# Streamed columns, low parts and sums in the first third of a fused attention and token-mixer kernel

## The chip, the cores and the metric

The kernel runs on one core of one Trainium2 chip. The metric is the device time of one execution in microseconds (us); smaller is better. A core has five engines that run side by side and wait for each other by semaphores: TensorE (PE in the profile, with its weight loads shown as PEld), VectorE (DVE), ScalarE (ACT), GpSimd (POOL) and SyncE (SP, which here only issues DMAs). Each engine works through its own instructions in the order in which the program wrote them.

## The reference

One block of two parts with adaptive layer norms, on x of 2048 tokens by 448 features, all in fp32:

```python
mod = (silu(c) @ w_mod).reshape(6, 448)          # sa, ca, ga, sb, cb, gb
h = layernorm(x) * (1 + ca) + sa
q, k, v = h @ wqkv                               # 16 heads of 28
phi = lambda t: where(t > 0, t + 1, exp(t)) + 1e-6
kv = einsum("hsd,hse->hde", phi(k), v);  z = phi(k).sum over tokens
o = phi(q) @ kv / (phi(q) . z + 1e-6)
x = x + ga * (o @ wo)
h = layernorm(x) * (1 + cb) + sb
u = gelu(einsum("sd,sf->df", layernorm(h), w1) + b1)   # mixes over tokens
x = x + gb * (einsum("df,fs->sd", u, w2) + b2)
```

## The kernel before

The tokens are cut into 16 tiles of 128 (NT = 16). To keep fp32 accuracy on TensorE, a matrix is split into a high part, rounded to the short format fp32r, and a low part, the rest. A product is then three matmuls: high by high, high by low, low by high. The helper `split` makes both: ScalarE copies to fp32r (line L79 of the profile), VectorE subtracts (L80).

The work in the order of the program:

- **Start.** The modulation columns `1 + ca` and `sa` are made first, since they scale the weights. `col_mm` (L211) does this on TensorE: a piece of `w_mod` is the stationary operand, and one column of 128 numbers (a part of silu(c), or a column of ones) is streamed past it. `col_out` (L218) copies the result out of PSUM. `keep_warm` (L176) runs matmuls whose result nobody reads. `w_high` and `w_low` scale the projection weights and split them.
- **The pipeline over tiles**, after some tiles done by hand ahead of it: a loop over t from 4 to 15. On TensorE an iteration holds `project(t+1)` (ten matmuls, x by the scaled key weights), `close(t)` (an eleventh that brings in mean and shift), a small transpose for tile t+1, `a_outer(t-4)` (eleven matmuls that add up normed x by phi(k) in four PSUM banks `cacc`), and from t = 10 on `a_q` (a query projection). For these the other engines make: the parts `hh`, `hl` of transposed x (`a_split(t+3)`), the statistics of a tile (`a_stats(t+3)`), exp and relu of the keys (`a_exp(t)`, tiles `ek`, `rk`), `pk` (`a_pk(t)`, L400), its parts `pkh`, `pkl` (`a_pk_parts(t-1)`, L454 to L465), the normed x `xn` and its parts `xh`, `xl` (`a_high(t-2)`, `a_low(t-2)`, L435 to L443). The four parts of a scaled query weight are made in iterations 4 to 8 too (`w_high(0, ..)`, `w_low(0, ..)`, `row_part(0, ..)`).
- **Low parts by DMA.** For tiles 2 to 12, `pkl` and `xl` are not made by VectorE: ScalarE writes minus the high part, and a DMA issued on POOL adds the full tile to it in memory (`accum_op=ALU.add`). The helper `low` (L426) holds that choice for `xl`.
- **The sum of phi(k)** over tiles goes into two tiles, `pksum[0]` and `pksum[1]`. Tiles 2, 4, .. 12 (`SUM_DMA`) are added to the first by a DMA on POOL (L463), the others to the second by VectorE (L465).
- **Behind the loop** come the last `a_outer` calls, `zp` (two matmuls that turn the summed phi(k), split as `zh`, `zl`, into z), `zb` (its copy by ScalarE), `csum` (L654, L655), `kvb` (L664), the query projections left over, then the normalized attention output and the two token-mixing products, which fill the time from about 125 us to the end.

Most tiles live in one pool of 74 slots in SBUF (`slot`), handed out again in the order in which they came free; who writes a tile waits for the last reader of the slot's tile before. A second pool of 27 (`tslot`) lies behind the constants, so that the size of the unused constant `space` moves it. `moving` takes a tile's columns from 16 on, so that the streamed operands begin 64 bytes into their slot. In the program as built, the slots begin at byte 1152 of a partition, the second pool at byte 170304. `load_x` and `load_xt` fetch x and its transposed form; iteration t issues those of tile t+5.

Of the kernel before, what the change touches and what calls it, by code (L numbers as in the profile page):

```python
# [8 lines left out]
F32 = mybir.dt.float32  # L9
# [5 lines left out]
P = 128  # L15
# [12 lines left out]
Q_EARLY = {10: 0, 11: 1, 12: 2, 13: 3, 14: 4}  # L28
ACT_STATS = range(5)
RING = 6  # L30
SUM_DMA = (2, 4, 6, 8, 10, 12)
ROWS = 98
DVE_LOW = (0, 1, 13, 14, 15)
AHEAD = 8
# [13 lines left out]
def block_kernel(ctx: ExitStack, tc: tile.TileContext, x, xt, wqkv, wo, w1, b1, w2, b2, c, wmod, wfirst, out):  # L48
# [16 lines left out]
    def slot(name, w=D, dt=F32, parts=P):  # L65
        return slots.tile([parts, w], dt, name=name, tag="slot", padded_shape=[P, 512])
# [11 lines left out]
    def split(full, hi, lo):  # L78
        nc.scalar.activation(hi, full, AF.Copy)  # L79
        nc.vector.tensor_sub(lo, full, hi.bitcast(F32))  # L80
# [12 lines left out]
                            pattern=[[0, 4], [-DH, 4], [0, DH]], channel_multiplier=1)  # L93
    nc.gpsimd.affine_select(out=m3, in_=m3, compare_op=ALU.is_ge, fill=0.0, base=DH - 1,
                            pattern=[[0, 4], [DH, 4], [0, DH]], channel_multiplier=-1)
    cst.tile([P, 96], F32, name="space")
    mhalf = cst.tile([P, 2], F32, name="mhalf")
    nc.vector.memset(mhalf, -0.5)
    roots = cst.tile([P, 2], F32, name="roots")
# [20 lines left out]
    def load_x(t):  # L120
        X[t] = slot(f"x{t}")
        nc.sync.dma_start(X[t], xf[t * P:(t + 1) * P, :])
# [53 lines left out]
    def keep_warm(n):  # L176
        for i in range(n):
            nc.tensor.matmul(warm[:, :P], ones, ones, start=True, stop=True)
# [30 lines left out]
                                           op0=ALU.mult, op1=ALU.add)  # L209

    def col_mm(ps, a, b, first, last):  # L211
        for ch in range(4):
            n = P if ch < 3 else 64
            nc.tensor.matmul(ps[:n, ch:ch + 1], a[:, ch * P:ch * P + n], b, start=first and ch == 0, stop=last,
                             skip_group_check=True)
        nc.tensor.matmul(ps[64:, 3:4], a[:, 384:D], b, start=False, stop=last, skip_group_check=True)

    def col_out(j, ps):  # L218
        col[j] = cst.tile([P, 4], F32, name=f"col{j}")
        if j == 1:  # L220
            nc.vector.tensor_scalar_add(col[j], ps[:, :4], 1.0)
        else:
            nc.vector.memset(col[j], 0.0)
            nc.vector.tensor_copy(col[j][:, :3], ps[:, :3])
            nc.vector.tensor_copy(col[j][:64, 3:4], ps[:64, 3:4])
# [92 lines left out]


    heads, mv, xn = {}, {}, {}  # L320

    def b_square(src, nm, acc, name):
        junk = slot(f"sq{name}")
        nc.scalar.activation(junk, src, AF.Square, bias=nm, accum_out=acc)

    def a_stats(t):
        mv[t] = cst.tile([P, 3], F32, name=f"mv{t}")
        ve = small.tile([P, 2], F32, name=f"ve{t}", tag="ve")
        if t in ACT_STATS:
            junk = slot(f"ja{t}")  # L330
            sm = small.tile([P, 3], F32, name=f"as{t}", tag="as")
            nc.scalar.activation(junk, X[t], AF.Identity, accum_out=sm[:, 0:1])
            nc.scalar.activation(sm[:, 1:2], sm[:, 0:1], AF.Copy, scale=-1.0 / D)
            b_square(X[t], sm[:, 1:2], sm[:, 2:3], f"s{t}")
            nc.gpsimd.tensor_scalar_mul(mv[t][:, 0:1], sm[:, 0:1], 1.0 / D)
            nc.gpsimd.tensor_scalar(ve, sm[:, 2:3].to_broadcast([P, 2]), 1.0 / D, EPS, op0=ALU.mult, op1=ALU.add)
            nc.gpsimd.tensor_tensor(mv[t][:, 1:3], ve, roots, op=ALU.pow)
            return
        b6 = small.tile([P, 6], F32, name=f"st{t}", tag="st")
        nc.vector.bn_stats(b6, X[t])  # L340
        nc.vector.bn_aggr(mv[t][:, 0:2], b6)
        nc.vector.tensor_scalar_add(ve, mv[t][:, 1:2].to_broadcast([P, 2]), EPS)
        nc.gpsimd.tensor_tensor(mv[t][:, 1:3], ve, roots, op=ALU.pow)
# [11 lines left out]
    def a_transpose(t0, n=1):  # L355
        ps = bank(f"rw{t0}")
        for i in range(n):
            tps[t0 + i] = ps[:, i * P:(i + 1) * P]
            nc.tensor.transpose(tps[t0 + i][:ROWS], rowst[(t0 + i) % RING][:, :ROWS].bitcast(F32), ident)

    def a_copy(t):
        nc.scalar.activation(heads[t][1][64:ROWS, 384:], tps.pop(t)[64:ROWS], AF.Copy)

    def a_split(t):
        heads[t] = (slot(f"hh{t}", 512, F32R), slot(f"hl{t}", 512, F32R))
        split(XT[t], *heads[t])
        XT[t] = None

    pps = {}

# [21 lines left out]
    def a_exp(t, ps):  # L392
        eks[t] = (slot(f"ek{t}"), slot(f"rk{t}"))
        nc.scalar.activation(eks[t][0], ps, AF.Exp, scale=mv[t][:, 2:3])
        nc.scalar.activation(eks[t][1], ps, AF.Relu, scale=mv[t][:, 2:3])
# [27 lines left out]
    xss, pks = {}, {}  # L423
    pksum = []

    def low(t, lo, full, hi):  # L426
        if t in DVE_LOW:
            nc.vector.tensor_sub(lo, full, hi.bitcast(F32))
        else:
            nc.scalar.activation(lo, hi.bitcast(F32), AF.Copy, scale=-1.0)  # L430
            nc.gpsimd.dma_start(lo, full, accum_op=ALU.add)

    def a_high(t):
        h = slot(f"xn{t}")
        nc.vector.tensor_scalar(h, X[t], mv[t][:, 0:1], mv[t][:, 2:3], op0=ALU.subtract, op1=ALU.mult)  # L435
# [4 lines left out]
    def a_low(t):  # L440
        h = xn.pop(t)
        hi, lo = xss[t]
        nc.vector.tensor_sub(hi[:, D:], h[:, 384:D], hi[:, 384:D].bitcast(F32))  # L443
        low(t, lo, h[:, :384], hi[:, :384])

    pkf = {}

    def a_pk(t, ps):
        pkf[t] = phi_k(t, ps, tslot if t < 2 else slot)

    def a_pk_parts(t):
        pk = pkf.pop(t)
        hi, lo = moving(slot, f"pkh{t}"), moving(slot, f"pkl{t}")
        nc.scalar.activation(hi, pk, AF.Copy, bias=1e-6)  # L454
        if t in DVE_LOW:
            nc.vector.scalar_tensor_tensor(lo, pk, 1e-6, hi.bitcast(F32), op0=ALU.add, op1=ALU.subtract)  # L456
        else:
            nc.scalar.activation(lo, hi.bitcast(F32), AF.Copy, scale=-1.0, bias=1e-6)
            nc.gpsimd.dma_start(lo, pk, accum_op=ALU.add)
        if t < 2:  # L460
            pksum.append(pk)
        elif t in SUM_DMA:
            nc.gpsimd.dma_start(pksum[0], pk, accum_op=ALU.add)  # L463
        else:
            nc.vector.tensor_add(pksum[1], pksum[1], pk)  # L465
        pks[t] = (hi, lo)
# [20 lines left out]
    col_acc(1)  # L487
    a_split(0)
    col_mm(pc, macc.pop(1), one, False, True)
    keep_warm(2)  # L490
    col_out(1, pc)
    for ch in range(4):
        w_high(1, ch)
# [30 lines left out]
    a_stats(5)  # L524
    row_out(1)
    a_transpose(2, 2)
    project(4, 1, "kp")
    a_high(0)
    a_copy(2)
# [26 lines left out]
    for t in range(4, NT):  # L556
        if t + 1 < NT:
            project(t + 1, 1, "kp")
        kp = close(t, 1)
        if t + 1 < NT:  # L560
            a_transpose(t + 1)
        if t == 9:
            row_sum(0)
            row_bias(0)
        a_outer(t - KV_LAG)
        if t in Q_EARLY:
            a_q(Q_EARLY[t])
        if t == 12:
            mp = mod_sum2(2)
        if 4 < t < NT - 2:  # L570
            a_rows(t + 2)
        if 5 <= t < 9:
            w_low(0, t - 5)
            row_part(0, t - 5)
        if 7 < t + 3 < NT:
            a_stats(t + 3)
        a_phi_q(t in Q_EARLY)
        if t + 1 < NT:
            a_copy(t + 1)
        a_exp(t, kp)  # L580
        a_pk_parts(t - 1)
        highs = HIGH_AT.get(t, (t - 2,))
        for i in highs[:1]:
            a_high(i)
        a_pk(t, kp)
        for i in highs[1:]:
            a_high(i)
        for i in highs:
            a_low(i)
        if t + 3 < NT:  # L590
            a_split(t + 3)
        if 4 <= t < 8:
            w_high(0, t - 4)
        if t == 9:
            row_out(0)
        if t == 12:
            mod_out(2, mp)
        if t + 5 < NT:
            load_x(t + 5)
            load_xt(t + 5)  # L600
        if 7 <= t < 11:
            mod_part(2, t - 7)
        if t == 11:
            mod_split(2)
        for j, i in MOD_AT.get(t, ()):
            mod_part(j, i)
        if t == 5:
            load_mod(2)
        if t in (7, 9):
            load_mod(4 if t == 7 else 3)  # L610
        if t == 10:
            load_qkv(2, tslot)
        if t == 8:
            for g in range(4):
                w = tslot(f"wo{g}", parts=G)
                nc.sync.dma_start(w, wo[g * G:(g + 1) * G, :])
                wo_sb.append(w)
            b1c = cst.tile([P, NF], F32, name="b1c")
            nc.sync.dma_start(b1c, b1)
            b2c = cst.tile([P, NT], F32, name="b2c")  # L620
            nc.sync.dma_start(b2c, b2)
        if t >= 13:
            nc.vector.tensor_mul(wo_sb[t - 13], wo_sb[t - 13], mods[2][:G])
        load_to(PRE_LOAD.get(t, 0))
# [12 lines left out]
        mod_part(3, i)  # L637
    split_to(2)
    a_outer(NT - 2)
    zp = bank("zp")  # L640
    for i, pk in enumerate(zs):
        nc.tensor.matmul(zp[:, :D], ones_r, pk, start=(i == 0), stop=(i == 1))
    a_outer(NT - 1)
    zb = tslot("zb")
    nc.scalar.activation(zb, zp[:, :D], AF.Copy, bias=S * 1e-6)
    mod_split(4)
# [564 lines left out]
```

## Time and profile before

| what | value |
|---|---|
| time, median of 3 runs | 459.51 us (458.79 to 460.73) |
| time of the profiled execution | 459.63 us |
| its span, first to last instruction | 457.9 us |
| so around the span | 1.7 us |
| mean granted TensorE clock | 0.989 |
| busy: TensorE, VectorE, ScalarE, GpSimd | 445.3, 350.7, 274.7, 114.4 us |

How to read it: a row of the timeline gives start, duration, engine, line, operation, output<-inputs, shape, and in brackets how long the engine had sat idle and who ended that. Matmuls overlap in the record: one of 448 columns shows about 0.36 us, and the next begins about 0.20 us after it, so the distance between starts is what counts. The view of stretches gives for each window its length, the busy time of PE, PEld, DVE, ACT and POOL with the number of instructions, the granted clock, the share of the DMA engines' time that was busy, and GB/s. The view of waits gives who waited for whom, in total us, times, and the longest. The chain is the work that ended last, followed back, in order of time: start, us, what.

### The profile page before, as it was taken

Reading aid. Unit: us, or ns where it says so; the run is one execution under the profiler, and the core shown is the slowest. Engines: PE = TensorE matmul, PEld = TensorE weight load, DVE = VectorE, ACT = ScalarE, POOL = GpSimd, SP = SyncE. Lnnn points to the kernel's source line nnn. Section 1 sums busy time; section 2 is a strip of 40 time slices with the busy share of each in tenths; the row PEclk is TensorE's granted clock in tenths of the full one; section 3 lists DMA queues with packets and bytes.
Section 4 is the critical chain, followed back from the end, with each engine's and each line's share of the span. In section 5 each row is a group of like instructions: output and inputs, shape, how many; then the busy total and the mean of one; then the engine's idle time right before and its main releaser. Section 6 shows DMA issues by size and latency. Waiting matters only on the chain.

```text
span 457.9 us, 7383 instructions
## 1 busy us (share of the span) xinstructions
PE 445.3 (97%) x2364; PEld 409.0 (89%) x2364; DVE 350.7 (77%) x783; ACT 274.7 (60%) x596; POOL 114.4 (25%) x213
## 2 busy tenths in 40 slices
PE   8987899999999999999999999999999999999996
PEld 7865689998989999999999999999999999999996
DVE  3777887758999889988549766739696878978872
ACT  4888887775775676767665453426564446446531
POOL 3536554430003345444510000000100202302101
PEclk8899899999999999999999999999999999999999
DMA  7957999667300001422324544326895958967333
GB/s 263 379 164 164 212 255 280 100 121 235 110 1 1 1 23 25 116 49 47 83 100 153 178 158 149 100 87 192 254 236 113 195 168 175 217 164 143 52 87 61
DMA packets 59718, 64.25 MB, mean 140 GB/s; under 512 B 5344, under 2 KB 50208, under 8 KB 59680
## 3 DMA queue, kind: packets, MB, share of 16 engines
q1 hardware_dynamic: 51616, 51.17, 36.1%
q0 software_dynamic: 8064, 12.62, 17.5%
q8 instruction: 18, 0.29, 0.3%
q14 instruction: 20, 0.16, 0.1%
HBM read 46.57 MB, written 7.34 MB: 118 GB/s over the span
## 4 chain that ended last, share of the span: by engine, by line
PE 91%; ACT 3%; DMA 3%; DVE 1%; issue 1%; SPq 0%; POOL 0%
PE y L967 14%; PE up L775 10%; PE up L777 10%; PE up L776 10%; PE op L724 9%; PE qp L383 7%; PE y L968 7%; PE cacc L480 7%; PE kp L383 6%; PE yp L775 2%; PE yp L777 2%; PE yp L776 2%; PE tq L708 2%; DMA xl<-xn 1%; DMA xt<-in_xt_dram 1%
## 5 line engine op out<-in xcount | busy, mean ns | idle before, releaser
L775 PE MATMUL up<-h2h,ph 128*128 128x448 f32 x224 | 81.4, 363 | 0.0
L777 PE MATMUL up<-h2h,pl 128*128 128x448 f32 x224 | 81.2, 363 | 0.0
L776 PE MATMUL up<-h2l,ph 128*128 128x448 f32 x224 | 80.8, 361 | 0.0
L79 ACT ACTIVATE ph<-pr 128x512 fp32r<-128x512 f32 (+1 forms) x60 | 32.9, 569 | 24.0 <-PE up L776 17.7
L80 DVE TENSOR_TENSOR pl<-pr,ph 128x512 fp32r<-128x512 f32 (+1 forms) x60 | 36.3, 615 | 14.2 <-ACT ph L79 10.3
L777 PEld LDWEIGHTS up<-h2h,pl 128*128 128x128 f32 x224 | 42.0, 188 | 3.2
L776 PEld LDWEIGHTS up<-h2l,ph 128*128 128x128 f32 x224 | 42.0, 187 | 3.0
L775 PEld LDWEIGHTS up<-h2h,ph 128*128 128x128 f32 x224 | 42.1, 188 | 2.5
L929 POOL DMA_DIRECT2D a<-a x12 | 10.7, 936 | 114.2 <-PE yp L777 96.9
L987 POOL DMA_DIRECT2D out_dram<-yt x12 | 10.5, 874 | 81.8 <-DVE yt L978 53.5
L383 PE MATMUL kp<-wh,hh 128*128 128x448 f32 x64 | 25.1, 398 | 1.6 <-ACT hh L79 1.0
L480 PE MATMUL cacc<-pkh,xh 128*128 128x448 f32 x64 | 24.9, 389 | 0.7 <-ACT pkh L454 0.7
L973 ACT ACTIVATE cc<-y 128x448 f32<-128x448 f32 x18 | 9.8, 546 | 24.9 <-PE y L968 24.9
L724 PE MATMUL op<-wph,pth 112*128 112x448 f32 x64 | 24.7, 385 | 0.0
L480 PE MATMUL cacc<-pkl,xh 128*128 128x448 f32 x64 | 23.9, 374 | 0.2 <-DVE pkl L456 0.2
L383 PE MATMUL qp<-wh,hh 128*128 128x448 f32 x64 | 23.5, 367 | 0.0
L724 PE MATMUL op<-wpl,pth 112*128 112x448 f32 x64 | 23.4, 365 | 0.0
L724 PE MATMUL op<-wph,ptl 112*128 112x448 f32 x64 | 23.4, 365 | 0.0
L480 PE MATMUL cacc<-pkh,xl 128*128 128x448 f32 x48 | 18.0, 375 | 3.6 <-DMA xl<-xn 3.6
L712 ACT ACTIVATE pth<-tq 112x512 fp32r<-112x512 f32 x16 | 9.6, 600 | 19.6 <-PE tq L708 19.6
L775 PE MATMUL yp<-uw,qw 128*128 128x448 f32 x54 | 19.9, 369 | 0.0
L777 PE MATMUL yp<-uw,qw 128*128 128x448 f32 x54 | 19.7, 364 | 0.0
(246 smaller groups left out, 1329.2 us busy)
## 6 DMA issues: line engine op xcount, KB each, us to landing
pr<-in_B_w_dram SPq DMA_DIRECT2D x48, 256.0 KB, 3.0
a<-in_B_w_dram SPq DMA_DIRECT2D x24, 256.0 KB, 5.0
a<-in_B_w_dram SPq DMA_DIRECT2D x24, 192.0 KB, 5.1
xt<-in_xt_dram SPq DMA_DIRECT2D x16, 256.0 KB, 4.9
x<-in_A_x_dram SPq DMA_DIRECT2D x16, 224.0 KB, 4.5
wm<-in_B_wmod_dram SPq DMA_DIRECT2D x16, 196.0 KB, 4.8
wr<-in_qkv_dram SPq DMA_DIRECT2D x12, 224.0 KB, 5.4
out_dram<-x SPq DMA_DIRECT2D x12, 224.0 KB, 2.0
```

The lines of the kernel that those rows point to most:

```text
L79: nc.scalar.activation(hi, full, AF.Copy)
L80: nc.vector.tensor_sub(lo, full, hi.bitcast(F32))
L383: nc.tensor.matmul(ps[:, :D], a[:, ch * P:(ch + 1) * P], b, start=(n == 0), stop=False)
L480: nc.tensor.matmul(cacc[ch][:, :D], a[:, s], b, start=(t == 0 and i == 0), stop=(t == NT - 1 and i == len(todo) - 1))
L724: nc.tensor.matmul(opb[t][:, :D], a[:, s], b, start=(n == 0), stop=(n == 11))
L775: nc.tensor.matmul(ps[:, :D], hi[:, sl], mh, start=first, stop=False)
L776: nc.tensor.matmul(ps[:, :D], hi[:, sl], ml, start=False, stop=False)
L777: nc.tensor.matmul(ps[:, :D], lo[:, sl], mh, start=False, stop=last)
L929: nc.gpsimd.dma_start(w, a, accum_op=ALU.add)
L967: nc.tensor.matmul(ps[:, :D], h[:, s], w, start=opens and r == 0, stop=False, skip_group_check=True)
L968: nc.tensor.matmul(ps[:, :HD], l[:, s], wh, start=False, stop=closes and r == PAIRS - 1, skip_group_check=True)
L987: nc.gpsimd.dma_start(of[t * P:(t + 1) * P, :], ysum.pop(t), accum_op=ALU.add)
```

## The change

Six edits, all in the part before 115 us:

1. `col_mm` streams 128 equal columns in the place of one (the same column, broadcast), into 128 PSUM columns for each piece; `col_out` reads the first of each. `keep_warm(2)` behind it becomes `keep_warm(5)`.
2. `xl` of tiles 2 to 12 is made by VectorE (`hi` subtracted from the full tile), as for the other tiles; the copy by ScalarE and the DMA on POOL go.
3. All of tiles 2 to 12 are summed by DMA, even ones into `pksum[0]`, odd ones into `pksum[1]`; the VectorE additions of 3, 5, 7, 9 and 11 go.
4. In the loop, the high part of x for tile t+3 is made by ScalarE right behind `a_exp(t)` (before: near the end of the iteration), the low part by VectorE right behind `a_pk(t)`.
5. x and its transposed form are fetched seven tiles ahead in the place of five; those of tiles 9 and 10, and one load of modulation weights, are issued before `project(4)`. The scratch outputs of the statistics on ScalarE share one slot, `junk`.
6. `a_outer(15)` comes ahead of the two `zp` matmuls. The unused constant shrinks by 192 bytes a partition.

```diff
-SUM_DMA = (2, 4, 6, 8, 10, 12)
+FETCH = 7
+SUM_DMA = range(2, 13)
...
-    cst.tile([P, 96], F32, name="space")
+    cst.tile([P, 48], F32, name="space")
...
     def col_mm(ps, a, b, first, last):
+        b = b.to_broadcast([P, P])
         for ch in range(4):
             n = P if ch < 3 else 64
-            nc.tensor.matmul(ps[:n, ch:ch + 1], a[:, ch * P:ch * P + n], b, start=first and ch == 0, stop=last,
-                             skip_group_check=True)
-        nc.tensor.matmul(ps[64:, 3:4], a[:, 384:D], b, start=False, stop=last, skip_group_check=True)
+            nc.tensor.matmul(ps[:n, ch * P:(ch + 1) * P], a[:, ch * P:ch * P + n], b, start=first and ch == 0,
+                             stop=last, skip_group_check=True)
+        nc.tensor.matmul(ps[64:, 384:512], a[:, 384:D], b, start=False, stop=last, skip_group_check=True)
 
     def col_out(j, ps):
         col[j] = cst.tile([P, 4], F32, name=f"col{j}")
+        ps = ps.rearrange("p (c n) -> p c n", n=P)[:, :, 0]
         if j == 1:
-            nc.vector.tensor_scalar_add(col[j], ps[:, :4], 1.0)
+            nc.vector.tensor_scalar_add(col[j], ps, 1.0)
...
+    junk = slot("junk")
 
     def b_square(src, nm, acc, name):
-        junk = slot(f"sq{name}")
-        nc.scalar.activation(junk, src, AF.Square, bias=nm, accum_out=acc)
+        dst = junk if name[0] == "s" else slot(f"sq{name}")
+        nc.scalar.activation(dst, src, AF.Square, bias=nm, accum_out=acc)
...
-            junk = slot(f"ja{t}")
...
+    def a_split_high(t):
+        heads[t] = (slot(f"hh{t}", 512, F32R), slot(f"hl{t}", 512, F32R))
+        nc.scalar.activation(heads[t][0], XT[t], AF.Copy)
+
+    def a_split_low(t):
+        nc.vector.tensor_sub(heads[t][1], XT[t], heads[t][0].bitcast(F32))
+        XT[t] = None
...
-    def low(t, lo, full, hi):
-        if t in DVE_LOW:
-            nc.vector.tensor_sub(lo, full, hi.bitcast(F32))
-        else:
-            nc.scalar.activation(lo, hi.bitcast(F32), AF.Copy, scale=-1.0)
-            nc.gpsimd.dma_start(lo, full, accum_op=ALU.add)
...
-        low(t, lo, h[:, :384], hi[:, :384])
+        nc.vector.tensor_sub(lo, h[:, :384], hi[:, :384].bitcast(F32))
...
         elif t in SUM_DMA:
-            nc.gpsimd.dma_start(pksum[0], pk, accum_op=ALU.add)
+            nc.gpsimd.dma_start(pksum[t % 2], pk, accum_op=ALU.add)
...
-    keep_warm(2)
+    keep_warm(5)
...
     a_transpose(2, 2)
+    load_xt(9)
+    load_x(9)
+    load_mod(2)
+    load_xt(10)
+    load_x(10)
     project(4, 1, "kp")
...
         a_exp(t, kp)
+        if t + 3 < NT:
+            a_split_high(t + 3)
         a_pk_parts(t - 1)
...
         a_pk(t, kp)
+        if t + 3 < NT:
+            a_split_low(t + 3)
         for i in highs[1:]:
             a_high(i)
         for i in highs:
             a_low(i)
-        if t + 3 < NT:
-            a_split(t + 3)
...
-        if t + 5 < NT:
-            load_x(t + 5)
-            load_xt(t + 5)
+        if t + FETCH < NT:
+            load_x(t + FETCH)
+            load_xt(t + FETCH)
...
-        if t == 5:
-            load_mod(2)
...
     a_outer(NT - 2)
+    a_outer(NT - 1)
     zp = bank("zp")
     for i, pk in enumerate(zs):
         nc.tensor.matmul(zp[:, :D], ones_r, pk, start=(i == 0), stop=(i == 1))
-    a_outer(NT - 1)
```

More of the change, by code (lines that the diff above doesn't have):

```diff
@@ L362, in a_copy @@
         nc.scalar.activation(heads[t][1][64:ROWS, 384:], tps.pop(t)[64:ROWS], AF.Copy)
+    def a_split_high(t):
[4 more added lines that the diff above has]
+        XT[t] = None
     def a_split(t):
-        heads[t] = (slot(f"hh{t}", 512, F32R), slot(f"hl{t}", 512, F32R))
-        split(XT[t], *heads[t])
-        XT[t] = None
+        a_split_high(t)
+        a_split_low(t)
     pps = {}
```

## The prediction

> **What bounds the kernel now.** First the page: its shares of the chain that ended last.
>
> ```profile
> PE 91%; ACT 3%; DMA 3%; DVE 1%; issue 1%; SPq 0%; POOL 0%
> ```
>
> TensorE sets the end, so a saving counts only where TensorE stands still or runs slowly. Next, the view of stretches, to find where that is.
>
> ```profile
> 10.00:15.00 5.00, 4.72 (x13) 4.18 (x14) 4.51 (x8) 4.01 (x9) 0.00 (x0) 0.50 1.03 375
> ...
> 40.00:45.00 5.00, 3.28 (x14) 2.34 (x14) 3.94 (x12) 4.63 (x10) 2.86 (x5) 1.00 1.03 187
> ...
> 50.00:55.00 5.00, 2.73 (x9) 2.13 (x9) 3.94 (x12) 4.65 (x9) 1.96 (x4) 0.82 1.06 275
> ```
>
> The seventh number is the granted clock. It is half from 10 to 15 us, where TensorE runs the first key projections; from 40 to 55 us TensorE is busy for little over half the time, and at 50 to 55 the clock sags again. Third, the chain through that part, in order of time.
>
> ```profile
> 10.28 8.84 PE kp L383 x30
> ...
> 45.88 6.73 DMA xl<-xn
> 52.61 0.04 issue
> 52.66 3.31 PE cacc L480 x9
> 55.97 2.39 PE kp L383 x10
> ...
> 60.88 2.03 PE kp L383 x10
> 62.91 0.21 PE kp L387
> 63.11 0.11 PE rw L359
> ...
> 65.38 2.20 PE cacc L480 x11
> ```
>
> Up to 52.6 us the DMA that finishes a low part of x is on the chain; behind it TensorE is. At full speed an iteration without extras is 2.03 + 0.21 + 0.11 + 2.20 = 4.55 us of TensorE. Right behind the DMA wait the same matmuls are slow: nine take 3.31 us where 9/11 of 2.20 is 1.80, and ten take 2.39 instead of 2.03. That is 1.51 + 0.36 = 1.87 us lost to the lower clock. Last, TensorE's own rows, for each stop.
>
> ```profile
> 25.09 0.32 PE L359 MATMUL rw<-ident,rowst 128*98 128x128 f32 x1 [0.48 <-POOL rowst L351]
> ...
> 39.55 0.37 PE L480 MATMUL cacc<-pkl,xh 128*128 128x448 f32 x1
> 40.93 0.47 PE L383 MATMUL kp<-wh,hh 128*128 128x448 f32 x1 [1.01 <-ACT hh L79]
> 41.24 0.36 PE L383 MATMUL kp<-wl,hh 128*128 128x448 f32 x1
> 41.66 0.47 PE L383 MATMUL kp<-wh,hl 128*128 128x448 f32 x1
> ...
> 43.91 0.36 PE L480 MATMUL cacc<-pkl,xh 128*128 128x448 f32 x1
> 45.55 0.47 PE L480 MATMUL cacc<-pkh,xl 128*128 128x448 f32 x1 [1.28 <-DMA xl<-xn]
> ...
> 50.02 0.37 PE L480 MATMUL cacc<-pkl,xh 128*128 128x448 f32 x1
> 52.66 0.47 PE L480 MATMUL cacc<-pkh,xl 128*128 128x448 f32 x1 [2.27 <-DMA xl<-xn]
> ```
>
> I count from start to start and take off 0.20 for the matmul itself: 1.18 us before 40.93 (ScalarE's `hh7`), 0.22 before 41.66 (VectorE's `hl7`), 1.44 before 45.55 and 2.44 before 52.66 (the DMAs of `xl2` and `xl3`).
>
> **Edits 2 and 4, low parts and order.** With `xl` made by VectorE the two DMA waits have no subject: 1.44 + 2.44 + 1.87 of clock = 5.75 us. With `hh7` right behind the exp and relu of tile 4 it is made ahead of two parts of phi(k) and two of x, four instructions of 0.5 to 0.6 us, so it is there before TensorE asks at 39.6; that is 1.18 + 0.22 = 1.40 us. What is late next? ScalarE loses the copy for `xl` in each iteration; VectorE gains a subtraction in each and loses an addition in every second one.
>
> ```profile
> 44.87 0.52 ACT L430 ACTIVATE xl<-xh 128x384 fp32r<-128x384 f32 x1
> ```
> ```profile
> 32.37 0.55 DVE L428 TENSOR_TENSOR xl<-xn,xh 128x384 fp32r<-128x384 f32 x1
> ...
> 48.97 0.62 DVE L465 TENSOR_TENSOR pk<-pk,pk 128x448 f32<-128x448 f32 x1
> ```
> ```profile
> 46.55:52.34 5.79, 3.83 (x20) 3.16 (x18) 4.73 (x13) 4.66 (x10) 3.48 (x4) 1.00 1.04 215
> ```
>
> This stretch is one iteration of VectorE (t = 6). ScalarE, busy 4.66, goes to 4.14, below TensorE's 4.55. VectorE, busy 4.73, goes to 4.73 - 0.62 + 0.55 = 4.66: 0.1 us over TensorE. An odd iteration has no addition and comes to the same 4.66. There are four of this kind (5 to 8, with the query weights); VectorE falls behind by 0.1 in each, and I charge 0.35 us. This holds only if VectorE's own idle time goes:
>
> ```profile
> DVE hl L80 <- ACT hh L79: 11.2, 12, 1.8
> ```
>
> Twelve times it waited for `hh`, 11.2 us in all, since ScalarE made `hh` behind `xh` and the copy. In the new order `hh` is done two instructions before VectorE wants it, and the wait moves to the cheaper end of the iteration. Between "all of it goes" (nothing) and "all of it stays" (11.2/12 = 0.9 us in each of four iterations, less the 0.35) the cost is 0 to 3.4 us; I stay near the lower end because the order on both queues puts a full instruction between.
>
> The other thing that can be late next is `pkl2`, still a DMA. It is issued at 37.11:
>
> ```profile
> 37.11 1.25 POOL L459 DMA_DIRECT2D pkl<-pk  x1 [1.55 <-DVE mv L341]
> ```
> ```profile
> DMA to landing us min/median/max: 3.2/4.8/6.4
> ```
>
> With the 0.35 us from the start (below) it is issued at 36.8 and lands at 41.6, at worst 43.2. TensorE wants it when `project(7)` is over: 39.55 - 0.35 + 0.20 for the last `outer(1)`, plus 2.03 + 0.21 + 0.11, is 41.75, and the second matmul of `outer(2)` takes it at 41.95. By the median nothing is lost, by the maximum 1.2 us, and then perhaps the clock too. Later `pkl` tiles have a whole iteration more. The Trainium skill, in DMA: Bandwidth & Descriptors, section Anatomy of one DMA — SWDGE (gpsimd) path, gives such a DMA 2.0 us and its bytes at 436 GB/s, by my estimate 2.5 us for 224 KB; by that it would land at 39.3 with time to spare and this risk would vanish. No row here is that short (3.2 at least), so the sum goes by the rows.
>
> **Edit 3.** Five VectorE additions of 0.62 go (counted above). On POOL eleven `xl` DMAs go and five for sums come, so its queue, where the reciprocal roots also wait, gets shorter. Nobody reads the sums before `zh`. What it does cost is time for which a slot is held, a rival below.
>
> **Edits 1 and 5, the start.** Thirty matmuls at half clock take 8.84 us; at 0.203 each they would take 6.1, but the scaled weights come from ScalarE and VectorE at their pace, so I give TensorE about 1.4 us. Hardly any of it arrives. ScalarE is the next to bind, and its only waits for TensorE in the start are these:
>
> ```profile
> 23.79 0.44 ACT L362 ACTIVATE hl<-rw 34x128 fp32r<-34x128 f32 x2 [0.19 <-PE rw L359]
> 24.54 0.54 ACT L284 ACTIVATE wrow<-rowb 34x448 fp32r<-34x448 f32 x1 [0.32 <-PE rowb L280]
> ```
>
> That is 0.51 us at most. And the transpose at 25.09 (quoted above) waits for POOL, whose chain hangs on ScalarE's statistics, not on TensorE; `project(4)` stands behind it and starts where it did. I take 0.35 us, between 0 and 0.51. The 128 wide columns themselves hide under the weight loads at full clock; at half clock they would make the start later (a rival). TensorE's pause ahead of 25.09 grows from 0.48 to about 1.6 us. A wait of 1.18 us at 40 left the clock at 1.00, one of 2.44 at 52 halved it, so this one is undecided: 0 to 1.5 us. The Trainium skill, TensorE: Matmul & The Clock Gate, section Why this matters for your kernels, warns only of pauses over about 3 us; here 2.44 was enough, so I keep the bound. The earlier fetches cost SP only issue time; no row shows TensorE waiting for x behind 10 us, so they gain nothing either.
>
> **Edit 6.**
>
> ```profile
> 110.72 0.36 PE L480 MATMUL cacc<-pkl,xh 128*128 128x448 f32 x1
> 111.76 0.47 PE L642 MATMUL zp<-zh,ones_r 128*128 128x448 f32 x1 [0.68 <-ACT zh L79]
> 112.42 0.47 PE L642 MATMUL zp<-zl,ones_r 128*128 128x448 f32 x1 [0.18 <-DVE zl L80]
> 112.73 0.36 PE L480 MATMUL cacc<-pkh,xh 128*128 128x448 f32 x1
> ```
>
> From 110.72 to 112.73 are 2.01 us, of which three matmuls need 0.60. `outer(15)` has its inputs by then and takes that time: 1.4 us saved. Its cover is that `zb`, now 0.8 us later, holds nobody up:
>
> ```profile
> 117.62 2.46 DVE L655 SCALAR_TENSOR_TENSOR cs<-zb,col,cs 128x448 f32<-128x448 f32 x4
> ...
> 119.80 2.42 PE L664 MATMUL kvb<-cs,wr 128*112 128x112 f32 x23
> ```
>
> VectorE gets to `csum` at 117.62 because of other work, the first is done at 118.2, and TensorE, 1.4 us earlier, asks at 118.4. Without that cover it costs up to 0.8.
>
> The smaller constant puts the second pool's streamed operands where those of the first pool are, at 64 past a multiple of 128 bytes. From the chain: the projections (second pool) take 203 ns a matmul, the outer products (first pool) 2.20/11 = 200. If the place is the reason, 352 projections gain 3 ns each, 1.1 us, and later products a little; if it is not, nothing, and it could be 1.1 the other way. I take a third, 0.4 us.
>
> **The sum.** 5.75 + 1.40 + 0.35 + 1.40 + 0.40 - 0.35 = 8.95 us off the profiled execution's 459.63 (span 457.9 and 1.7 around it; 0.12 above the median of 459.51, so no correction): 450.7 us. Behind 60 us TensorE has no stops to speak of, so what is won there stays won.
>
> **Rivals.** *Something else is late next.* VectorE keeps its waits (3.4 us), or `pkl2` is late and the clock falls with it (1.2 + 1.87 = 3.1): 453.8 to 454.1, both together 457.2. For it: VectorE has nothing to spare. Against: the new order and a lighter POOL. Chance 0.19.
>
> *The wide columns don't keep the clock up.* Then each of the first three groups of ten passes runs at half speed and the weights come later, by what ScalarE can't absorb, about 1 us, and the 0.35 is lost: 452.1. Chance 0.09.
>
> *Slower: engines wait for the summing DMAs.* Now every `pk` of tiles 2 to 12 holds its slot until its sum has landed, while fetches two tiles deeper and `junk` take five of the 74 slots, so that each comes round sooner. By counting slots in the order in which they come free, VectorE's or ScalarE's writes of iterations 8 to 10 get a `pk` slot whose DMA was issued about one iteration before. It happened already:
>
> ```profile
> ACT xl L430 <- DMA pk<-pk: 1.0, 1, 1.0
> ```
> ```profile
> DMA to landing us min/median/max: 3.2/4.8/6.7
> ```
>
> At the median the wait is 4.8 - 4.55 = 0.25 us, hidden by the iteration with which TensorE leads. At 6.7 it is 2.15, in four iterations 8.6, and with one fall of the clock (1.87) 10.5: 461.2 us. It decides from landings of about 6.3 us on, four in a row. Against: eleven `xl` DMAs leave the same DMA engines. Chance 0.10.
>
> *Part of this, gains and waits even out:* within 0.5% of before, 0.04.
>
> **How the numbers follow.** The forecast has 0.58. Its own range is 449.5 (no VectorE lag, the start's full 0.51, the whole 1.1) to 452.2 (the clock falls ahead of 25 us). The range over the cases goes down to 448.8, where the place of the streamed operands serves the later products as well by another 0.7, and up to both parts of the first rival together, 457.2; it leaves out the slower rival, most of the case of no change, and a small lower tail. A measurement of this kernel can tell about 0.5%, 2.3 us, from no change. Faster by more: 0.58 + 0.19 + 0.09 = 0.86, of which I move 0.02 to no change for mixed cases near 457: 0.84, 0.06, 0.10.
>
> **What would show it.** Right: granted clock near 1.00 from 10 to 15 us; no row of TensorE waiting for `xl`; `project(7)` starting straight behind `outer(1)`, near 39.3; TensorE busy over 4.8 of 5 us from 40 on; no stop between `outer(14)` and `outer(15)`; the pause ahead of 25.1 still there and longer. Wrong: waits for `pkl` at 42 us; VectorE waiting for `hh` or for a DMA of `pk`; a clock of 0.5 behind 25.9 us; `kvb` waiting for `cs`.

## The result and the profile after

| | before | changed |
|---|---|---|
| median | 459.42 us (458.79 to 460.73) | 452.48 us (451.52 to 455.27) |
| profiled execution, span | 459.63, 457.9 us | 451.52, 449.6 us |

The ratio is 0.9855, with a 95% interval of 0.9806 to 0.9904: the changed kernel is faster by 1.0 to 1.9%. The forecast was 450.7 us, its range 448.8 to 457.2.

TensorE holds the same share of the chain, and the DMAs a little less:

```profile
PE 91%; DMA 2%; POOL 2%; ACT 1%; DVE 1%; SPq 1%; issue 1%; ACTq 0%; POOLq 0%
```

The view of stretches, in the same windows as before and one further on (length, busy us of PE, PEld, DVE, ACT and POOL, granted clock, DMA share, GB/s):

```profile
10.00:15.00 5.00, 4.58 (x22) 3.26 (x21) 4.77 (x8) 3.95 (x9) 0.03 (x1) 1.00 1.04 386
...
40.00:45.00 5.00, 4.99 (x25) 4.28 (x25) 4.87 (x15) 4.87 (x11) 3.25 (x4) 1.00 1.05 219
...
50.00:55.00 5.00, 5.00 (x27) 4.51 (x26) 4.86 (x14) 4.56 (x10) 2.71 (x4) 1.00 1.05 262
...
70.00:75.00 5.00, 3.97 (x20) 3.40 (x19) 3.30 (x10) 3.62 (x8) 0.96 (x2) 1.00 0.65 121
```

The clock in the start is full, and TensorE is busy for all of 40 to 45 and of 50 to 55 us, where it stood still for 1.7 and 2.3 us. The price is seen beside it: from 40 to 45 us VectorE and ScalarE are both busy for 4.87 of 5 us, so they have next to nothing left to give there. The last row shows a hole of TensorE that the kernel before did not have:

```profile
70.00:75.00 5.00, 5.00 (x26) 4.61 (x25) 3.32 (x11) 3.80 (x8) 1.91 (x2) 1.00 1.10 268
```

The view of waits of the changed kernel names it, TensorE's rows first, then ScalarE's between 60 and 78 us:

```profile
PE rw L362 <- POOL rowst L354: 1.5, 1, 1.5
...
PE qp L393 <- ACT rq L416: 1.0, 1, 1.0
```
```profile
ACT eq L415 <- PE cacc L483: 3.1, 1, 3.1
ACT ek L404 <- DMA pk<-pk: 2.1, 1, 2.1
```

A query projection `qp` waits until ScalarE has read an earlier one out of PSUM (`eq`, `rq`), and ScalarE is late since it waited twice, at 65 us for the DMA of a phi(k) sum and at 71 us for something that this view puts down to TensorE. The timelines of POOL and ScalarE and the landing of the one sum issued between 60 and 66 us show what it was:

```profile
63.37 0.86 POOL L466 DMA_DIRECT2D pk<-pk  x1 [0.40 <-issue]
```
```profile
DMA to landing us min/median/max: 7.8/7.8/7.8
```
```profile
71.30 0.63 ACT L415 ACTIVATE eq<-qp,mv 128x448 f32<-128x448 f32 x1 [3.13 <-PE cacc L483]
```

63.37 + 7.8 = 71.2, and `eq` starts 0.1 us later. In the built program `eq` has the slot in which phi(k) of tile 8 lay until its sum had landed, and the `ek` that starts at 64.95 has that of tile 7. The engine that the wait of `eq` names had little to do with it. In another execution of the same kernel (the run called `e5_after_again` below) the same wait is named outright, and is longer:

```profile
ACT eq L415 <- DMA pk<-pk: 4.0, 1, 4.0
```

### The profile page after: what moved, and what is told of

Read it like the earlier page. It is cut to its first block, busy times and chain, and to the rows that moved or that the text cites. A ratio compares the mean times of both kernels' runs of the same rounds, so it can differ in the third digit from the quotient of the medians.

```text
span 449.6 us, 7344 instructions
## 1 busy us (share of the span) xinstructions
PE 441.2 (98%) x2370; PEld 406.1 (90%) x2370; DVE 352.1 (78%) x789; ACT 268.9 (60%) x585; POOL 109.0 (24%) x207
## 4 chain that ended last, share of the span: by engine, by line
PE 91%; DMA 2%; POOL 2%; ACT 1%; DVE 1%; SPq 1%; issue 1%; ACTq 0%; POOLq 0%
PE y L975 14%; PE up L783 10%; PE up L785 10%; PE up L784 10%; PE op L732 9%; PE cacc L483 7%; PE qp L393 7%; PE y L976 7%; PE kp L393 5%; PE yp L783 2%; PE yp L785 2%; PE yp L784 2%; PE tq L716 2%; DMA wr<-in_qkv_dram 1%; DMA x<-in_A_x_dram 1%
## 5 line engine op out<-in xcount | busy, mean ns | idle before, releaser
L995 POOL DMA_DIRECT2D out_dram<-yt x12 | 10.5, 872 | 84.4 <-DVE yt L986 55.9
L393 PE MATMUL kp<-wh,hh 128*128 128x448 f32 x64 | 23.6, 374 | 0.4 <-DVE wh L265 0.2
L783 PE MATMUL yp<-uw,qw 128*128 128x448 f32 x54 | 20.0, 370 | 0.0
L785 PE MATMUL yp<-uw,qw 128*128 128x448 f32 x54 | 19.7, 364 | 0.0
L784 PE MATMUL yp<-uw,qw 128*128 128x448 f32 x54 | 19.6, 363 | 0.0
```

The lines of the kernel that those rows point to most:

```text
L393: nc.tensor.matmul(ps[:, :D], a[:, ch * P:(ch + 1) * P], b, start=(n == 0), stop=False)
L783: nc.tensor.matmul(ps[:, :D], hi[:, sl], mh, start=first, stop=False)
L784: nc.tensor.matmul(ps[:, :D], hi[:, sl], ml, start=False, stop=False)
L785: nc.tensor.matmul(ps[:, :D], lo[:, sl], mh, start=False, stop=last)
L995: nc.gpsimd.dma_start(of[t * P:(t + 1) * P, :], ysum.pop(t), accum_op=ALU.add)
```

## Experiments

The theory after the first look had three parts: edit 2 brings nearly all of the gain and edit 4 makes it whole; `zp` is worth 1.4 us; and the gain that is missing lies in the stop at 71 us, which the new sums make. Rivals: the wide columns or the place of the constants matter, or the stop has another cause.

**Edit 2 undone** (`e1_xl_by_dma`, from the changed kernel):

```diff
     def a_low(t):
...
-        nc.vector.tensor_sub(lo, h[:, :384], hi[:, :384].bitcast(F32))
+        if t in DVE_LOW:
+            nc.vector.tensor_sub(lo, h[:, :384], hi[:, :384].bitcast(F32))
+        else:
+            nc.scalar.activation(lo, hi[:, :384].bitcast(F32), AF.Copy, scale=-1.0)
+            nc.gpsimd.dma_start(lo, h[:, :384], accum_op=ALU.add)
```

> The changed kernel with the low parts of normed x of tiles 2 to 12 made by ScalarE and a DMA again, all other edits kept. Theory A (these DMAs were the stop): TensorE waits for xl again between 40 and 55 us, with a fall of the clock behind the longer wait; 3 to 6 us over the changed kernel's 452.5, so 455 to 459. Rival B (the gain came from the clock at the start, the order and the fetches; the earlier fetches would let the DMAs land in time): within 1 us of the changed kernel, no TensorE wait for xl.

Measured: 461.30 us, ratio to before 1.0034 (1.0009 to 1.0058). All the other edits together, without this one, make the kernel slightly slower. Its waits and stretches:

```profile
PE cacc L487 <- DMA xl<-xn: 6.6, 2, 4.4
```
```profile
45.00:50.00 5.00, 3.11 (x10) 2.81 (x11) 4.25 (x13) 4.89 (x11) 4.28 (x5) 0.76 1.01 177
```

That is above the range that was expected. There are again two waits for `xl`, 6.6 us in place of 3.55 by this view, but they are not the same two: TensorE stops for 4.42 us ahead of 46.89 and for 2.16 ahead of 71.55, where before it stopped ahead of 45.55 and 52.66. What follows: edit 2 is what takes the wait away, and with the other edits in place and this one missing the wait is longer.

**Edit 2 alone** (`e2_xl_by_vector`, from the kernel before, the one line of `a_low` above).

> The kernel before with one edit: the low parts of normed x by VectorE. Theory A: the two DMA waits (1.44 and 2.44 us) and the slow clock behind them (1.87) go, but VectorE still waits for the late high part of transposed x and now has more to do, so 3 to 5.5 us of the 5.75 stay: 454 to 456.5. Rival B: VectorE becomes the bound, within 1.5 us of before (458 to 461).

Measured: 454.62 us, 0.9909 (0.9879 to 0.9938). **Edit 4 alone** (`e3_order`, from before, with the two helpers of the change in the place of `a_split`):

```diff
         a_exp(t, kp)
+        if t + 3 < NT:
+            a_split_high(t + 3)
...
         a_pk(t, kp)
+        if t + 3 < NT:
+            a_split_low(t + 3)
...
-        if t + 3 < NT:
-            a_split(t + 3)
```

> The kernel before with one edit: the high part of transposed x made right behind exp and relu, its low part right behind phi(k). Theory A: the stop of 1.2 us at 40.9 us goes, but TensorE then asks for xl sooner and waits that much longer for its DMA, so hardly anything arrives: 0 to 1.5 us off, 458 to 459.5. Rival: the order alone also moves the DMAs' issue ahead and gives 3 us or more.

Measured: 460.71 us, 1.0031 (1.0007 to 1.0055), a little slower, where a small gain was expected. The wait for `xl` grew:

```profile
PE cacc L487 <- DMA xl<-xn: 5.1, 2, 3.3
```

With `hh` ahead of it on ScalarE, the first copy for `xl` starts at 41.02 us where it started at 39.83, and its DMA is issued at 41.91 in place of 40.92. **Edits 2 and 4** (`e4_xl_order`, from before):

> The kernel before with both edits, low parts by VectorE and the new order. Theory A: these two carry 6 to 7 us of the gain (5.75 + 1.40 less some lag of VectorE): 452.5 to 453.5, and TensorE has no stop over 0.5 us from 36 to 60 us. Rival: without the sums moved to the DMA and the earlier fetches VectorE, with five additions more, keeps TensorE waiting: 455 or more.

Measured: 453.35 us, 0.9874 (0.9859 to 0.9889), as expected. So by the medians edit 4 costs 1.3 us alone and brings 1.3 us behind edit 2, where the two intervals still touch. The traces agree: from the start of the first outer product to the sixth one it is 59.46 - 30.94 = 28.52 us with edit 2 alone and 59.47 - 32.15 = 27.32 with both, 1.20 less. The order is worth something only when no DMA hangs behind ScalarE's copy.

**The changed kernel again** (`e5_after_again`, no edit), to see its spread.

> The changed kernel itself, timed beside its variants on one chip: 451.5 to 453, from 452.5. Some executions lie 1 to 3 us above the fastest; by my reading these have one fall of the clock (mean 0.996) behind the pause at 25 us or the stop at 71 us.

Measured: 452.49 us (451.34 to 455.45), 0.9854 (0.9823 to 0.9885). Its profiled execution took 455.1 us; TensorE's stop there and the stretch behind it:

```profile
74.13 0.47 PE L393 MATMUL qp<-wh,hh 128*128 128x448 f32 x1 [2.67 <-ACT rq L416]
```
```profile
75.00:80.00 5.00, 5.00 (x19) 4.50 (x18) 3.70 (x10) 4.10 (x9) 1.79 (x2) 0.66 0.22 38
```

Here the sum of tile 8 landed 8.8 us after its issue. The stop is 1.6 us longer than in the first profile, and the clock of 0.66 in the 5 us behind it costs another 5.00 x (1 - 0.66) = 1.7 us: 3.3 of the 3.6 us between the two executions. Of the ten executions here and in the result, five had a mean clock of 0.999 or 1.0 and took 451.3 to 452.1 us, five had 0.995 or 0.996 and took 452.8 to 455.5. Of the slower five only this one has a trace; that the long stop made the others slow too is a guess from their clock.

**Edit 1 undone** (`e6_one_column`): `col_mm` streams one column again, `keep_warm(2)`.

> The changed kernel with the first edit undone (one streamed column, two warming matmuls). Theory A (the start is held by ScalarE's statistics and POOL, the wide columns bring little): clock 0.5 from about 9 to 15 us again, and 0 to 0.6 us more than the changed kernel. Rival B (the clock at the start is a main part of the gain): 1.4 to 2.7 us more.

Measured: 451.86 us, 0.9827 (0.9805 to 0.9849), not slower. Its clock in the start is low again, and behind the pause at 25 us too:

```profile
10.00:15.00 5.00, 5.00 (x19) 4.01 (x18) 4.51 (x8) 3.94 (x8) 0.00 (x0) 0.75 1.06 392
25.00:30.00 5.00, 4.73 (x17) 4.21 (x18) 2.55 (x7) 2.37 (x6) 2.48 (x7) 0.66 1.02 281
```

In all nine traces with edit 1 the clock is 1.00 from 5 to 15 us. In the five without it, it is 0.50, 0.76, 0.81 and 0.75 from 10 to 15 us, but 1.00 in `e4_xl_order`: the full clock goes with edit 1, but one streamed column does not always lose it. The time shows no gain from it. This profiled execution took 453.11 us, its four others 451.67 to 452.13; how those four came by their time no trace here shows.

**`zp` first again** (`e7_zp_first`): `a_outer(15)` moved back behind the `zp` matmuls.

> The changed kernel with the two zp matmuls ahead of the last outer products again: TensorE waits for zh and zl as before, 1.4 us more than the changed kernel (1.2 to 1.6). Rival: the later zb held up kvb and ate up to 0.8 of it, then 0.6.

Measured: 455.34 us, 0.9898 (0.9877 to 0.992), 2.85 us over `e5_after_again`, twice what was expected. The traces give the smaller number: from 93.9 us, where both are alike, to the start of `kvb` it is 116.76 - 93.94 = 22.82 us here and 115.31 - 93.91 = 21.40 in `e5_after_again`, a difference of 1.42. In the medians the long stop seems to be mixed in: four of these six executions had a clock of 0.996, and the traced one of them stops for 2.7 us. That is not all of it, since the two at 0.999 and 1.0 took 453.74 and 454.53 us, against 451.34 to 451.98 for the three of `e5_after_again`; where the rest comes from no trace here shows.

**The constant at its old size** (`e8_space96`):

> The changed kernel with the unused constant at its old size, so that the second pool's streamed operands lie at a multiple of 128 bytes again. Theory A (the place costs the projections 3 ns a matmul, and in the changed kernel the late products with the same pool lost some): 0.4 to 1.1 us more than the changed kernel, and 203 to 206 ns from start to start in the projections. Rival: the place does nothing, within 0.2 us and 201 ns.

The second pool then lies where it lay before. Measured: 452.63 us, 0.9848 (0.9823 to 0.9873), no difference in the median. In the trace the place is seen. First the chain of the changed kernel, then that of `e8_space96`:

```profile
121.40 2.02 PE qp L393 x10
...
126.30 2.41 PE op L732 x12
```
```profile
121.88 2.06 PE qp L393 x10
...
126.85 2.47 PE op L732 x12
```

From the projection at 74.99 to the last of the `op` products at 208.78 the changed kernel takes 133.79 us, and this one from 75.25 to 209.76 takes 134.51: 0.72 more. The spans are 449.6 and 450.3. The six executions here spent 1.7 to 3.5 us outside their spans, so a median of six can hide that much.

**Fewer sums by DMA** (`e9_even_sums`), the first test of the stop:

```diff
-SUM_DMA = range(2, 13)
+SUM_DMA = (2, 4, 6, 8, 10, 12)
```

> The changed kernel with one part undone: phi(k) of the odd tiles 3 to 11 is added by VectorE again, and only the even tiles' sums go by DMA. Theory (the sums of two tiles in a row hold their phi(k) slots for 6 to 9 us, and the exponentials of a later tile wait for one of these slots at about 69 us, which stops TensorE near 71 us for 1.0 to 2.7 us and halves the clock behind it when the stop is long): tile 8's sum is still there, so a wait of ACT for a phi(k) slot may stay, but with half the traffic its DMA lands in 4.5 to 6 us and the stop of qp behind rq falls below 0.5 us; VectorE gets five additions of about 0.6 us, which it has time for behind 60 us only. Time 451.0 to 452.5, a steadier spread than the changed kernel's 451.3 to 455.4. Rival (VectorE was the engine that needed the relief): TensorE waits for pkl, xl or hl written by VectorE before 60 us, 1 to 3 us in sum, time 453 to 455.

Measured: 451.08 us (450.54 to 451.28), 0.9815 (0.9802 to 0.9828). Every one of its executions lies below the fastest one seen of the changed kernel (451.34), and all have a clock of 1.0. Its stretch at 70 us, and the landing of the sum of tile 8:

```profile
70.00:75.00 5.00, 5.00 (x27) 4.66 (x27) 4.73 (x12) 4.42 (x9) 1.02 (x1) 1.00 0.78 215
```
```profile
DMA to landing us min/median/max: 6.4/6.4/6.4
```

TensorE's row `qp <- rq` is gone. The landing was expected at 4.5 to 6 us and took 6.4; ScalarE still waits 1.3 us for it, and that is short enough to reach nobody: `eq` starts at 70.50 in place of 71.30, the `ek` ahead of it no longer waits for the sum of tile 7, and TensorE comes to `qp` 0.85 us later, at 72.16. VectorE took the five additions back without a wait that matters (`hl` 0.5 us in sum, which was 0.2). The changed kernel's intervals (0.9806 to 0.9904, and 0.9823 to 0.9885 in `e5_after_again`) overlap with this one. Those of the next two runs, which were timed beside it and sum every tile by DMA, do not (0.9849 and 0.9841 at the least). With the trace and the spread they decide that the step is real: without the five added sums the stop is gone. How they make it is less clear, since the four loads of the value weights go out later in this run too, at 66.02 in place of 62.05 us.

**Fetch depth back to five** (`e10_fetch5`):

```diff
-FETCH = 7
+FETCH = 5
...
-    load_xt(9)
-    load_x(9)
-    load_mod(2)
-    load_xt(10)
-    load_x(10)
...
+        if t == 5:
+            load_mod(2)
```

> The changed kernel with x and xt of tile t+5 fetched in step t again instead of t+7 (the one shared scrap tile for the squares is kept): four slots more are free between steps. Theory (a slot held by a summing DMA stops ACT at 65 to 71 us): with four free slots the exponentials at 64 and 71 us no longer wait for the DMA of a sum, the stop of qp behind rq goes, and the time is 450.5 to 451.8, if x is still there in time; x is fetched five steps of about 4.6 us ahead, and a load of x takes less than that. Rival (the further fetch is what feeds the faster first stage): VectorE or ACT waits for x's or xt's DMA in 25 to 60 us and TensorE behind them, 453 to 456. Second rival: the stop at 71 us has another cause than slots and stays, time 452 to 453.

Measured: 453.03 us, 0.9866 (0.9849 to 0.9882). The expectation failed: with four slots more the stop is still there.

```profile
72.76 0.47 PE L393 MATMUL qp<-wh,hh 128*128 128x448 f32 x1 [1.02 <-ACT rq L416]
```

The sum of tile 8 was issued at 64.94 and landed after 6.5 us, at 71.4; `eq` starts at 71.55. The wait of the `ek` at 64 us is gone, as expected, but one of 2.49 us for `hh` has come in its place:

```profile
66.86 0.64 ACT L369 ACTIVATE hh<-xt 128x512 fp32r<-128x512 f32 x1 [2.49 <-issue]
```

In the built program this `hh` has the slot of phi(k) of tile 7, whose sum was issued at 59.02 and landed after 7.8 us, at 66.8; and `eq` has the slot of tile 8 here too. So four more free slots do not take the stop away: they change which tile meets the late sum. Nothing waits for x, so within what this measures the deeper fetch brings nothing and costs nothing.

**Loads of the value weights three tiles later** (`e11_late_wr`), to take the transfers of 60 to 64 us out of the sum's way:

```diff
-        if t == 10:
+        if t == 13:
             load_qkv(2, tslot)
```

> The changed kernel with the four loads of the value projection's weights (wr2) issued three tiles later, behind the phi(k) sum of tile 8. Theory (the sum's DMA of tile 8 lands in 7.8 to 8.8 us because the loads at 60 to 64 us share the DMA engines with it, and the slot that it holds stops ACT and then TensorE): that landing falls to about 5 us, the stop of qp behind rq falls below 0.5 us, and the time is 450.5 to 451.5 and steadier; the weights are first read far behind, so nothing waits for them. Rival (the landing is long because of the sums before it, not because of the loads): landing and stop stay, time 452 to 453; or the later loads take slots that are then missing elsewhere and the stop moves behind 80 us.

Measured: 453.37 us (451.73 to 456.54), 0.9877 (0.9841 to 0.9912). The landing of tile 8's sum is 8.9 us, and the stop 2.86.

```profile
DMA to landing us min/median/max: 8.9/8.9/8.9
```
```profile
74.13 0.74 PE L393 MATMUL qp<-wh,hh 128*128 128x448 f32 x1 [2.86 <-ACT rq L416]
```

But the edit moved the loads in the program and not in time. SyncE had nothing else to issue in between. First the changed kernel, then this run:

```profile
62.05 2.04 SPq L144 DMA_DIRECT2D wr<-in_qkv_dram  x4
```
```profile
62.03 2.08 SPq L144 DMA_DIRECT2D wr<-in_qkv_dram  x4
```

So this run repeats the changed kernel and does not test its theory; neither the expectation nor its rival is decided. The other traces bear on it. In the six that sum every tile by DMA and issue these loads 1.3 to 1.9 us ahead of tile 8's sum (the changed kernel twice, `e6_one_column`, `e7_zp_first`, `e8_space96` and this run), the sum lands after 7.8 to 9.0 us. In the other eight, which issue them behind it, it lands after 5.4 to 6.7, and two of these, `e1_xl_by_dma` (6.2) and `e10_fetch5` (6.5), sum every tile by DMA too. Nor do fewer sums make every landing short: with the even ones alone, that of tile 6 took 7.0 us in `e9_even_sums`, 8.4 in `e3_order` and 8.2 in `e4_xl_order`. That loads issued just ahead of a sum lengthen its landing fits these traces; no run moves the loads alone, so it is not shown.

**Where the start's gain went** (`e12_even_sums_project4`): `e9_even_sums` with `project(4)` put into the pause at 25 us.

```diff
-    a_transpose(2, 2)
     load_xt(9)
...
     project(4, 1, "kp")
+    a_transpose(2, 2)
```

> The changed kernel with the odd tiles' phi(k) sums on VectorE again (as in the run before, 451.1) and, new, project(4) put ahead of the transposes of tiles 2 and 3, whose rows TensorE waits for at 25 us (1.50 us, a chain of small POOL operations). Question: where the faster start went. Theory (the start is set by the chain of ACT and POOL that makes the rows of tiles 0 to 3, so TensorE's faster matmuls ahead of it only lengthen the pause; what work of TensorE fits into the pause is gained, until ACT or VectorE bind): the wait of rw for rowst goes, the first exponential starts about 1 us earlier, and since ACT and VectorE are busy for 4.87 of 5 us in 40 to 45 us, 0.5 to 1.2 us of it reach the end: 450.0 to 450.6. Rival (from 28 us on ACT and VectorE set the pace, not TensorE): the pause goes and comes back as waits for hl, pkh or xl between 28 and 50 us, time 450.8 to 451.5.

Measured: 450.67 us (450.5 to 451.12), 0.9803 (0.9784 to 0.9822): by the median the fastest here, and not to be told from `e9_even_sums`. The pause of 1.50 us is gone from TensorE's rows. A wait of 0.78 stands in its place, and the one ahead of the first outer product stays (0.68 in `e9_even_sums`):

```profile
25.64 0.38 PE L362 MATMUL rw<-ident,rowst 128*98 128x128 f32 x2
...
27.32 0.68 PE L397 MATMUL kp<-wrow,hl 98*128 98x448 f32 x2 [0.78 <-ACT hl L365]
...
31.78 0.47 PE L483 MATMUL cacc<-pkh,xh 128*128 128x448 f32 x1 [0.72 <-ACT pkh L457]
```

The first outer product starts at 31.78, no earlier than the 31.51 of `e9_even_sums`. The time of 450.67 us lies between the two ranges, but the mechanism of the rival holds: the chain of this run has no engine but ScalarE and VectorE in it from 25 to 37 us, so they set the pace there.

## Why the prediction was right, and where it was off

**Edits 2 and 4: 5.75 + 1.40 - 0.35 = 6.80 us. Right.** Between the start of the first outer product and the sixth one, before and changed:

```profile
31.71 0.47 PE L480 MATMUL cacc<-pkh,xh 128*128 128x448 f32 x1 [0.68 <-ACT pkh L454]
```
```profile
31.20 0.47 PE L483 MATMUL cacc<-pkh,xh 128*128 128x448 f32 x1 [0.65 <-ACT pkh L457]
```
```profile
57.99 2.21 PE cacc L483 x11
```

The chain of before has that sixth one at 65.38: 33.67 us became 26.79, 6.88 less. By the same measure edit 2 alone gives 33.67 - 28.52 = 5.15 us and edits 2 and 4 together 6.35; the last 0.53 comes with the other edits, and which of them brings it was not taken apart. TensorE has no row that waits for `xl`, and `project(7)` starts straight behind `outer(1)`, at 39.23 (39.3 was forecast):

```profile
39.04 0.36 PE L483 MATMUL cacc<-pkl,xh 128*128 128x448 f32 x1
39.23 0.36 PE L393 MATMUL kp<-wh,hh 128*128 128x448 f32 x1
```

The term for VectorE was a little too large: TensorE waits 0.2 us for an `hl`, once, where 0.35 was charged, and of the seven waits for `hh`, 6.9 us, that VectorE had between 25 and 75 us one is left:

```profile
DVE hl L372 <- ACT hh L369: 1.8, 1, 1.8
```

`pkl2`, the other late candidate, landed 3.4 us after its issue, at the short end of the row that the forecast used, and nobody waited. The Trainium skill (DMA: Bandwidth & Descriptors, Anatomy of one DMA — SWDGE (gpsimd) path) would have it in 2.5 us by the estimate of the prediction; the sums, of the same size and queue, took 3.8 to 9.0 us in these runs, so by that rule the stop at 71 us would not exist, and the measurement decides.

**The start: 0.35 us. Not to be seen.** The transpose behind the pause moved from 25.09 to 24.93, but it stands at 24.64 in `e2_xl_by_vector` and at 25.85 in `e4_xl_order`, which both have the old start: executions differ by more than the edit brings. That the pause grows was right (1.50 us). That the clock might fall behind it did not happen in the two traces of the changed kernel.

**`zp`: 1.40 us. Right.** The chain, changed kernel:

```profile
95.80 11.01 PE cacc L483 x55
106.81 0.40 PE zp L651 x2
107.21 2.00 PE qp L393 x10
...
112.03 3.29 PE kvb L672 x32
```

Before, the outer products began at 102.27 and `qp` behind `zp` at 115.09. The lead is 6.47 us ahead of this place and 7.88 behind it: 1.41. `kvb`, feared to wait for `cs`, gives back 0.14 (3.29 for 3.15).

**The place of the operands: 0.40 us. Right in the trace, not in the median.** From 60 us on ten projection matmuls took 2.03 to 2.07 us before and take 2.00 to 2.02 where nothing stops them, and `e8_space96` puts 0.72 us on it from 75 to 209 us. Behind `kvb` the lead grows from 123.11 - 115.32 = 7.79 us to the spans' 8.3, so about 0.5 us there; between the outer products at 58 us and those at 96 us some is hidden under the loss below.

**What failed: the price of the summing DMAs.** The prediction had their mechanism as its slower rival, with the right trigger ("landings of about 6.3 us on") and close to the right place (ScalarE waits in iterations 10 and 11, where 8 to 10 were named), but put it into the sum at nothing, and as a rival at 10.5 us for four long waits in a row. It came in between. At 58 us the lead is 65.38 - 57.99 = 7.39 us, at 96 us 6.47. One wait reaches TensorE, of 1.0 us. The ten matmuls behind it take 2.28 us in the chain in place of 2.00: behind a wait the first one counts with its whole 0.47 us, the nine others with 0.20 each. The clock is full.

```profile
72.51 2.28 PE qp L393 x10
```

In the long form the wait is 2.7 to 2.9 us, with 1.7 of clock behind it in `e5_after_again` and `e11_late_wr`.

The argument against it ("eleven `xl` DMAs leave the same DMA engines") was the wrong step: without them the four sums issued between 48 and 64 us still landed after 6.2 to 7.8 us, where the longest of before was 6.7. Why they land so late stays open. The sum of 8.95 us stands against 8.11 between the two profiled executions, 459.63 - 451.52, and 6.94 between the medians. The gap from 8.11 to the medians is probably that stop in its long form, since half of the executions have the lower clock that goes with it where it was traced. With the 0.92 us lost between 58 and 96 us added, 8.11 becomes 9.03, very near the sum. That is in part luck: the start brought nothing that can be seen, and other terms brought a little more than they were given.

## What to carry to other kernels

In this kernel a DMA that reads a tile holds its slot until it lands, so moving an addition from an engine to a DMA frees the engine and can make the next writer of that slot wait for the slowest landing, not the median one. Look for it where an engine's wait is put down to another engine that had long been done, and compare the start with the landing of whatever last used the memory. And take edits apart before crediting them: the order of ScalarE's work cost 1.3 us by itself and brought 1.3 us once the DMA behind it was gone, and a clock that is full in the start bought nothing that these runs can tell, where TensorE did not set the pace. Last, look at issue times before reading a result: an instruction moved in the program has not moved in time when its engine had nothing to do in between.

## What the hardware showed unexpectedly

The same accumulating DMA of 224 KB landed anywhere from 3.1 to 9.0 us after its issue in these runs; what lengthens it was not isolated. The clock behind the pause of about 1.5 us at 25 us stayed at 1.00 in `e2_xl_by_vector` (1.50 us) and in the changed kernel (1.50), but was 0.66 over 25 to 30 us in `e3_order` (1.47) and `e6_one_column` (1.50); in `e7_zp_first` it stayed at 1.00 behind 2.00 us. What decides that stays open. The Trainium skill (TensorE: Matmul & The Clock Gate, HAM oscillation — how this bites in real kernels) has pauses over about 3.4 us as the limit; here a stop of 2.67 us and two of about 1.5 were followed by a clock of 0.66, and one of 2.00 us was not.
